# RWKV-6 attention with a gated feed-forward on one core: the input projections of the last two units made as one product of half matrices

## The chip, the core and the metric

The kernel runs on one core of a Trainium2 chip. The core has five engines that run side by side and wait for each other by semaphores: TensorE (matrix products; in profiles PE, and PEld for its loading of weights), VectorE (DVE), ScalarE (ACT), GpSimd (POOL) and SyncE (SP), which here only starts DMAs. TensorE reads from the on-chip memory SBUF and writes to the accumulators, PSUM[...]. The metric is the device time of one execution in microseconds; less is better.

## What is computed

Inputs r, k, v, w have the shape 4 (batch) x 8 (heads) x 768 (time) x 48. A recurrence over time gives y, and y, with the heads side by side, gives 3072 rows x of 384 numbers. They go through a feed-forward block with 2048 hidden features:

```python
for t in range(S):
    cur = np.einsum('bhd,bhe->bhde', u[None] * kt, vt)
    y[:, :, t] = np.einsum('bhd,bhde->bhe', rt, state + cur)
    state = wt[:, :, :, None] * state + np.einsum('bhd,bhe->bhde', kt, vt)
x = attn_out.transpose(0, 2, 1, 3).reshape(B * S, H * D)
h = x @ w_in                                             # 3072x384 by 384x2048
sp = np.maximum(h, 0.0) + np.log1p(np.exp(-np.abs(h)))   # softplus
g = h * erf(sp)
out = g @ w_out                                          # 3072x2048 by 2048x384
```

Everything is in 32-bit floats.

## The kernel before, in words

The work is cut into 12 steps (s = 0 to 11): 6 stretches of 128 time steps, each for two pairs of batches. A step makes the attention of 2 batches x 128 time steps; its 256 rows of x are called a unit and go through the feed-forward block behind it. For each unit there are

- the attention of its step. From step 5 on `attend_late` does it: products within a block of time by levels (`level_products`, L552, and `scale`, L328), their use on v (`from_own`, L584, in two halves, with the VectorE copy `seen`, L593, between them), the state products (`state_part`, L659), the sum `middle` (L736), and the part that comes through the state (`through_state`, L610). The last one copies the result from the accumulator `y` to the tile xT (ScalarE, L618 and L639) and moves 6 small pieces of it by DMA (L645). xT holds the unit's 384 inputs in three parts of 128 rows, 256 tokens wide.
- the input projection, `hidden` ("H"): 16 feature tiles of 128, three whole-array products each (L1027, weights 128x128 from w_in_sb, 256 columns), two feature tiles per accumulator, copied to h by ScalarE (L1036). 8 pieces of 6 products.
- the gating, in chunks of four feature tiles: softplus ("s", L983) and erf ("e", L987) on ScalarE, each with a load of its function table (1.28 us), and the product on VectorE ("m", L992).
- the output projection, `project_fast` ("P"), made by seven products of half matrices in place of eight: h and w_out are seen as 2x2 blocks. `blend` ("S", L1112 to L1118) makes four sums of blocks of h on VectorE; seven pieces of 8 products (L1135, 192 columns) follow, with evictions on ScalarE (L1141, L1146, L1149) and VectorE (L1155, L1160) and two output DMAs.

The order is written by hand: every engine performs its instructions in the order in which the program gives them out. In step s a "P" stands for the next output product of unit s - 3 and an "H" for the next piece of unit s - 1; they are put between the parts of the attention. `run_late` reads strings of such tokens; `LATE` holds those of step 11 by stage (front, near, 0, 1, 2, 3, 4). In step 11 the stages up to 1 hold the output products of unit 8, stage 2 the blend of unit 9, and stages 3 and 4 the 8 pieces of unit 10's input projection. Behind step 11 come the attention's last products, the output products of unit 9, the input projection of unit 11, and then the output products of units 10 and 11:

```python
from_own(s - 1, ready[s - 1][0], 1)
fence()
run_late(s, "s P")
from_own(s - 1, ready[s - 1][0], 0)
through_state(s - 1, xTs[s - 1])
run_late(s, "m ey m P s P P ep m P P P S H H s H ey m H H s H ep m H H")
run_late(s + 1, "s P ey m P s P P ep m P P P S")
run_late(s + 2, "P P P P P P P")
```

Products with fewer than 128 rows and columns (L552, L584, L610, L659) use a quarter of the array each: which rows follows from the partitions of the operands, which columns from the partitions of the result.

Of the kernel before, what the change touches and what calls it, by code (L numbers as in the profile page):

```python
# [11 lines left out]
FP32 = mybir.dt.float32  # L12
# [49 lines left out]
def kernel(  # L62
# [240 lines left out]
    def rows(e, n=D):  # L303
        return slice(e * EP, e * EP + n)
# [293 lines left out]
    def through_state(s, xT):  # L598

        c, in_t, _, _, S, _, _ = parts_of(s)  # L600
        for h, state in enumerate((S, middle)):
            if not (c or h):
                continue
            t = slice(h * HC, (h + 1) * HC)
            for j, q in ((0, 2), (1, 2), (1, 0), (0, 0)) if not s else np.ndindex(NJ, NP // 2):
                q = q if not s else 2 * q
                for e in range(NE):
                    for p in (q + e, q + 1 - e):
                        n = j * NP + p
                        nc.tensor.matmul(  # L610
                            y[at(e, p), e, p // 2, j, t],
                            lhsT=state[rows(e), n, :],
                            rhs=(in_t[:, 0, n] if s else first_pair(0, n))[rows(e), t],
                            start=False, stop=True, skip_group_check=True,
                        )

        y3 = att.tile([P, UNIT], FP32, name="y3", bufs=1)
        nc.scalar.copy(y3[:].rearrange("p (j t) -> p j t", j=NJ), y[:, 1, 1])  # L618
        parts = y[:, 0, 0], y[:, 0, 1], y[:, 1, 0]
        by_kk = [xT[:, kk, :].rearrange("p (j t) -> p j t", j=NJ) for kk in range(KT)]  # L620
        if not s:

            def hop():
                for kk in range(KT):
                    nc.tensor.matmul(
                        parts[kk], lhsT=apart[:, kk],
                        rhs=y3[:].rearrange("p (j t) -> p j t", j=NJ),
                        start=False, stop=True, skip_group_check=True,
                    )
                for kk in range(KT):  # L630
                    nc.scalar.copy(by_kk[kk], parts[kk])
                stages["l"](3, xT[:, KT - 1, 0:1], True)
                stages["l"](4)
                load_w(2)

            turns["hop"] = hop
            return
        for kk in range(KT):
            nc.scalar.copy(by_kk[kk], parts[kk])  # L639
        by_scalar = {(kk, 1) for kk in range(KT) if s <= DIRECT}  # L640
        for kk in range(KT):
            n = D // KT
            for e in range(NE):
                queue = nc.scalar if (kk, e) in by_scalar else nc.sync
                queue.dma_start(  # L645
                    out=xT[e * EP + D : (e + 1) * EP, kk, :],
                    in_=y3[e * EP + kk * n : e * EP + (kk + 1) * n, :],
                )
# [424 lines left out]
    def mix_weights():  # L1073
# [9 lines left out]
            engine.tensor_tensor(out=of, in0=a, in1=b, op=op)  # L1083
        yield

    blends, lanes = {}, {}

    def quarter(of, what):
# [8 lines left out]
    def blend(of, *parts):  # L1097

        if of not in blends:
            if of < n_steps - 1:  # L1100
                tiles = [room[:, n] for n in (1, 2, 3)]
            else:
                two = att.tile([P, 2, JP, C], FP32, name="rk1", bufs=1)
                one = ins.tile([P, JP, C], FP32, name="w")
                tiles = [x.rearrange("p n t -> p (n t)") for x in (two[:, 0], two[:, 1], one[:])]
            s1, s2, s4 = (x.rearrange("p (f t) -> p f t", t=C) for x in tiles)
            blends[of] = s1, s2, quarter(of, "21"), s4
        s1, s2, s3, s4 = blends[of]
        a = {what: quarter(of, what) if what not in lanes else lanes[what] for what in ("11", "12", "22")}
        for part in parts or (1, 2, 4, 3):  # L1110
            if part == 1:
                nc.vector.tensor_add(s1, s3, a["22"])  # L1112
            elif part == 2:
                nc.vector.tensor_sub(s2, s1, a["11"])
            elif part == 3:
                nc.vector.tensor_sub(s3, a["11"], s3)
            else:
                nc.vector.tensor_sub(s4, a["12"], s2)  # L1118

    def project_fast(s, gs):  # L1120
# [47 lines left out]
                nc.sync.dma_start(out=out[i * NJ, c, :, part], in_=o[0][:, part])  # L1168
        yield

    xTs, hids, projs = {}, {}, {}
    gated = [[] for _ in range(n_steps)]

# [28 lines left out]
    def in_order(s, k):  # L1202
# [3 lines left out]
        for what in order[k]:  # L1206
# [12 lines left out]
            "S2 S3 H k12y S4 H F", "s H ep m H H F G s H H H ep",  # L1219
        ),  # L1220
        n_steps - 1: (
            "s P", "m", "ey P m s P P ep P", "m P P", "S", "H H", "s H ey m H H s H ep H H"
        ),
    }
    USUAL = (
# [4 lines left out]
    def run_late(s, tokens, following=None):  # L1230

        for what in tokens.split():
# [5 lines left out]
                piece(hids, s - 1)  # L1238
            elif what == "F":
                next(following, None)  # L1240
            elif what == "G":
                mixing.send(nc.gpsimd)
            elif what == "s":
# [39 lines left out]
    with tc.manual_schedule(  # L1283
# [74 lines left out]
        s = n_steps  # L1358
        from_own(s - 1, ready[s - 1][0], 1)
        fence()  # L1360
        run_late(s, "s P")
        from_own(s - 1, ready[s - 1][0], 0)
        through_state(s - 1, xTs[s - 1])
        run_late(s, "m ey m P s P P ep m P P P S H H s H ey m H H s H ep m H H")
        run_late(s + 1, "s P ey m P s P P ep m P P P S")
        run_late(s + 2, "P P P P P P P")


# [94 lines left out]
```

## Time and profile before

| | us |
|---|---|
| median of 3 runs | 589.04 (588.01 to 589.31) |
| the profiled execution | 591.17 |
| its span, first to last instruction | 589.3 |
| TensorE busy | 582.3 |
| VectorE busy | 434.6 |
| ScalarE busy | 361.2 |
| GpSimd busy | 273.4 |
| one unit's input projection (96 records) | 20.9 |

The page of the profile gives busy time by engine, and the chain of work that ended last; the trace behind it can be asked for the instructions of any stretch in order of time. A row of such an answer gives the start in us from the first instruction, the duration, the engine, the line of the program, the operation, the tile that is written and those that are read, for TensorE the part of the array that is used (rows*columns), the shape, and how many instructions the row stands for. In square brackets stands the idle time of the engine ahead of it and what ended it; "issue" means that no other instruction did. A 32-bit product on TensorE leaves two records of loading and two of multiplying. The ends of products are modelled, so that rows overlap; starts are measured.

### The profile page before, as it was taken

What the parts mean: (1) busy time and instruction counts of PE and PEld (TensorE: products, weight loads), DVE (VectorE), ACT (ScalarE), POOL (GpSimd) and SP (SyncE); (2) the same over time, 40 slices, a digit from 0 to 9 for tenths busy, and PEclk for the clock granted to TensorE, in tenths of its full rate; (3) what the DMA queues carried; (4) which work ended last, traced back from release to release, by engine and by line L of the source; (5) the groups of instructions that cost most, each with busy time, mean ns of one, the idle gap of its engine ahead of it and who ended that gap; (6) DMA issues with size and microseconds to landing.
All of it is one profiled execution on the core that took longest, in us unless ns stands there. A gap on an engine that the chain in (4) does not pass through costs nothing.

```text
span 589.3 us, 16635 instructions
## 1 busy us (share of the span) xinstructions
PE 582.3 (99%) x7256; PEld 500.6 (85%) x7256; DVE 434.6 (74%) x523; ACT 361.2 (61%) x474; POOL 273.4 (46%) x313
## 2 busy tenths in 40 slices
PE   8899999999999999999999999999999999999997
PEld 6688887688668768998998998998898898898997
DVE  6775886899996899799799799799799525023140
ACT  3567878644544598756766766766766754746720
POOL 4557381702398479569369369369359000000000
PEclk9899999999999999999999999999999999999999
DMA  7577572440432514234334334333331300000000
GB/s 258 185 258 292 187 238 61 172 153 10 143 110 103 135 45 160 46 133 153 65 128 159 65 128 150 73 125 116 73 121 42 73 21 14 3 19 15 1 27 28
DMA packets 54081, 63.24 MB, mean 107 GB/s; under 512 B 35160, under 2 KB 40568, under 8 KB 52984
## 3 DMA queue, kind: packets, MB, share of 16 engines
q1 hardware_dynamic: 53624, 61.98, 33.2%
q8 instruction: 57, 0.93, 0.7%
q10 hardware_dynamic: 384, 0.20, 0.1%
q14 instruction: 16, 0.13, 0.1%
HBM read 52.39 MB, written 8.69 MB: 104 GB/s over the span
## 4 chain that ended last, share of the span: by engine, by line
PE 89%; DVE 8%; issue 1%; DMA 1%; POOL 0%; SPq 0%; DVEq 0%; POOLq 0%
PE m L1027 40%; PE m L1135 28%; PE m L1059 6%; PE pp L552 6%; PE y L584 2%; PE pp L659 2%; PE y L610 2%; DVE in L328 2%; PE m L862 1%; DVE words L467 1%; DVE rk L463 1%; DMA rest<-in_w_rows 1%; DVE sums L453 1%; PE pp L871 1%; DVE h L1016 1%
## 5 line engine op out<-in xcount | busy, mean ns | idle before, releaser
L1027 PE MATMUL m<-xT,w_in_sb 128*128 128x256 f32 x1152 | 256.8, 382 | 0.0
L1027 PEld LDWEIGHTS m<-xT,w_in_sb 128*128 128x128 f32 x1152 | 216.4, 190 | 30.5 <-ACT h L1036 0.3
L1036 ACT COPY h<-m 128x512 f32<-128x512 f32 x96 | 55.5, 578 | 83.1 <-PE m L1027 83.1
L328 DVE TENSOR_TENSOR in<-in,tot_sb 128x1024 f32<-128x1024 f32 (+1 forms) x55 | 74.6, 1357 | 15.9 <-PE pp L552 13.7
L463 POOL TENSOR_TENSOR rk<-words 128x528 f32<-128x528 f32 (+3 forms) x28 | 42.4, 1515 | 91.2 <-DVE sums L453 80.8
L467 POOL TENSOR_TENSOR words<-words,rest 128x528 f32<-128x528 f32 (+10 forms) x77 | 78.1, 1015 | 6.0
L1059 PE MATMUL m<-w_out_sb,h 128*128 128x384 f32 x192 | 64.3, 491 | 0.0
L1059 PEld LDWEIGHTS m<-w_out_sb,h 128*128 128x128 f32 x192 | 35.7, 190 | 23.5
L1135 PE MATMUL m<-mixed,h 128*128 128x192 f32 x288 | 51.1, 331 | 0.0
L983 ACT ACT_TABLE_LOAD x36 | 46.2, 1283 | 2.8 <-issue 2.1
L1135 PE MATMUL m<-w_out_sb,h 128*128 128x192 f32 x272 | 47.5, 329 | 0.0
L1135 PEld LDWEIGHTS m<-mixed,h 128*128 128x128 f32 x288 | 46.6, 190 | 0.9
L987 ACT ACT_TABLE_LOAD x36 | 46.2, 1283 | 1.6 <-DVE room L1118 1.1
L1135 PEld LDWEIGHTS m<-w_out_sb,h 128*128 128x128 f32 x272 | 44.3, 190 | 0.4
L1135 PE MATMUL m<-w_out_sb,room 128*128 128x192 f32 x256 | 44.2, 326 | 0.0
L552 PEld LDWEIGHTS pp<-in 48*64 48x64 f32 (+1 forms) x2368 | 33.4, 126 | 11.6 <-issue 6.0
L1135 PEld LDWEIGHTS m<-w_out_sb,room 128*128 128x128 f32 x256 | 42.0, 190 | 0.0
L992 DVE TENSOR_TENSOR h<-h,y 128x1024 f32<-128x1024 f32 x17 | 20.7, 1216 | 28.3 <-ACT y L987 28.1
L402 POOL TENSOR_TENSOR tot_sb<-tot_sb 128x256 f32<-128x256 f32 (+4 forms) x50 | 37.1, 742 | 3.8
L983 ACT ACTIVATE room<-h 128x1024 f32<-128x1024 f32 x36 | 38.1, 1057 | 0.4
L992 DVE TENSOR_TENSOR h<-h,pp 128x1024 f32<-128x1024 f32 x19 | 23.1, 1213 | 19.5 <-ACT pp L987 19.5
L552 PE MATMUL pp<-in 48*64 48x32 f32 (+1 forms) x2368 | 37.1, 212 | 0.2 <-DVE in L328 0.2
(147 smaller groups left out, 830.5 us busy)
## 6 DMA issues: line engine op xcount, KB each, us to landing
in<-in_rkw SPq DMA_DIRECT2D x8, 1024.0 KB, 5.7
words<-in_moe_w_in SPq DMA_DIRECT2D x16, 384.0 KB, 6.1
words<-in_moe_w_out SPq DMA_DIRECT2D x16, 384.0 KB, 5.8
words<-in_rk_rows SPq DMA_DIRECT2D x8, 768.0 KB, 6.4
w<-in_rkw SPq DMA_DIRECT2D x11, 512.0 KB
v<-in_v SPq DMA_DIRECT2D x12, 384.0 KB, 5.7
out<-o SPq DMA_DIRECT2D x23, 192.0 KB, 2.9
in<-in_rkw SPq DMA_DIRECT2D x7, 512.0 KB, 5.8
```

Of the source, the lines that this page charges most:

```text
L328: nc.vector.tensor_mul(halves, halves, view(tots[level - 1], 0, [[1, n], [2, nb], [0, half]]))
L402: nc.gpsimd.tensor_mul(new, pair[:, :, 0], pair[:, :, 1])
L463: engine.tensor_mul(terms[n], r[:, :, n:], k[:, :, : near - n])
L467: engine.tensor_mul(k[:, :, :m], k[:, :, :m], w[:, :, n : n + m])
L552: nc.tensor.matmul(to, lhsT=rk(1, n)[rows(e), s0 : s0 + m], rhs=right, start=True, stop=True,)
L983: nc.scalar.activation(sp_room, chunks[0], AF.Softplus)
L987: nc.scalar.activation(at, sp_room, AF.Erf)
L992: nc.vector.tensor_mul(h, h, at)
L1027: nc.tensor.matmul(ps[:, ff, :], lhsT=w_in_sb[:, g * FG + f + ff, kk * P : (kk + 1) * P], rhs=xT[:, kk, :], start=kk == 0, stop=kk == KT - 1,)
L1036: nc.scalar.copy(h[:, f : f + FT, :], ps[:])
L1059: nc.tensor.matmul(ps[j][:], lhsT=gs[g][:, f, j * C : (j + 1) * C], rhs=w_out_sb[:, g * FG + f, :], start=g + f == 0, stop=g == NG - 1 and ...
L1135: nc.tensor.matmul(to, lhsT=a[:, f], rhs=b[:, f], start=start and f == 0, stop=f == FG - 1, skip_group_check=True,)
```

## The change

Units 10 and 11 are projected together. Seen as 2x2 blocks, the inputs of w_in are halved (two halves of 192 rows), its features are halved (two groups of 8 tiles), and the tokens are the two units. The four block results are then made from seven products of blocks in place of eight, with sums of blocks made ahead:

- A half of the inputs is one of the first two 128-row parts and 64 rows of the third. A product of one pair of feature tiles is so made of 2 whole-array matmuls (L1281 of the new program) and 4 matmuls of 64 rows by 64 features on the four quarters of the array (L1288), all 256 columns wide. There are 7 x 4 of them.
- `join_weights` moves 64-row parts of w_in to the other rows (4 DMAs, SBUF to SBUF) and makes four sums of weight blocks on VectorE, one in step 11's near stage, one in stage 1 and two behind the step. `swap_rows` moves 64 rows of each unit's third part to the other rows (2 DMAs a unit), and `join_tokens` makes four sums of token blocks on VectorE.
- `hidden_of_two` makes the products, with two accumulators of `products` and the one named y, and puts the results together by ScalarE copies and VectorE sums. Gating is done by half chunks (`activate_pair`), with up to four activations between loads of a table.
- Step 11 holds no "H" and no blend any more. The blend of unit 9 comes behind the step, and of unit 9's seven output products the last two come behind the joint products. The six pieces of unit 11's xT are sent in another order, the third part first.

```diff
@@ -638,7 +638,7 @@
         for kk in range(KT):
             nc.scalar.copy(by_kk[kk], parts[kk])
         by_scalar = {(kk, 1) for kk in range(KT) if s <= DIRECT}
-        for kk in range(KT):
+        for kk in range(KT) if s < n_steps - 1 else np.roll(range(KT), 1):
             n = D // KT
             for e in range(NE):
                 queue = nc.scalar if (kk, e) in by_scalar else nc.sync
@@ -1083,6 +1083,11 @@
             engine.tensor_tensor(out=of, in0=a, in1=b, op=op)
         yield
 
+    def half_room(name, shape):
+        t = wide.tile(shape, I32, name=name, bufs=3 if name == "words" else 2)
+        t = t[:].rearrange("p a b two -> p (a b two)" if len(shape) == 4 else "p a b -> p (a b)")
+        return t.bitcast(FP32)
+
     blends, lanes = {}, {}
 
     def quarter(of, what):
@@ -1097,8 +1102,10 @@
     def blend(of, *parts):
 
         if of not in blends:
-            if of < n_steps - 1:
+            if of < n_steps - 2:
                 tiles = [room[:, n] for n in (1, 2, 3)]
+            elif of == n_steps - 1:
+                tiles = [half_room("words", [P, 2, DM, 2])[:, : FG * C] for _ in range(3)]
             else:
                 two = att.tile([P, 2, JP, C], FP32, name="rk1", bufs=1)
                 one = ins.tile([P, JP, C], FP32, name="w")
@@ -1168,6 +1175,175 @@
                 nc.sync.dma_start(out=out[i * NJ, c, :, part], in_=o[0][:, part])
         yield
 
+    def join_weights():
+
+        n = FG * P
+        tiles = [half_room("words", [P, 2, DM, 2]) for _ in range(3)]
+        s1, s2, s4 = (
+            (
+                t[:, :n].rearrange("p (f m) -> p f m", m=P),
+                t[:, n : n + n // 2].rearrange("p (f m) -> p f m", m=P),
+            )
+            for t in tiles
+        )
+        moved = [
+            half_room("rest", [P, 2, DM])[:, : n // 2].rearrange("p (f m) -> p f m", m=P)
+            for _ in range(2)
+        ]
+        a_rows, b_rows = (rows(e, EP) for e in range(NE))
+        thirds = [slice(kk * P, (kk + 1) * P) for kk in range(KT)]
+        for g in range(NG):
+            even, odd = (slice(g * FG + n, (g + 1) * FG, 2) for n in range(2))
+            nc.sync.dma_start(out=moved[g][a_rows], in_=w_in_sb[b_rows, even, thirds[2]])
+            nc.sync.dma_start(out=moved[g][b_rows], in_=w_in_sb[a_rows, odd, thirds[2]])
+
+        def whole(g, half):
+            return w_in_sb[:, g * FG : (g + 1) * FG, thirds[half]]
+
+        def rest(g, half, e):
+
+            if half == e:
+                return w_in_sb[rows(e, EP), g * FG + e : (g + 1) * FG : 2, thirds[2]]
+            return moved[g][rows(e, EP)]
+
+        def block(g, half):
+            return whole(g, half), [rest(g, half, e) for e in range(NE)]
+
+        def tile_of(t):
+            return t[0], [t[1][rows(e, EP)] for e in range(NE)]
+
+        s1, s2, s4 = (tile_of(t) for t in (s1, s2, s4))
+        a11, a12, a21, a22 = (block(g, half) for g in range(NG) for half in range(2))
+        turns["joint weights"] = {
+            "11": a11, "12": a12, "22": a22, "s1": s1, "s2": s2, "s3": a21, "s4": s4
+        }
+        yield
+        for out_, a, op, b in (
+            (s1, a21, ALU.add, a22), (s2, s1, ALU.subtract, a11),
+            (s4, a12, ALU.subtract, s2), (a21, a11, ALU.subtract, a21),
+        ):
+            nc.vector.tensor_tensor(out=out_[0], in0=a[0], in1=b[0], op=op)
+            for e in range(NE):
+                nc.vector.tensor_tensor(out=out_[1][e], in0=a[1][e], in1=b[1][e], op=op)
+            yield
+
+    def swap_rows(of):
+
+        if "swapped" not in turns:
+            t = att.tile([P, NH, HC], FP32, name="own")
+            t = t[:].rearrange("p n t -> p (n t)").rearrange("p (i t) -> p i t", t=UNIT)
+            turns["swapped"] = {n_steps - 2 + i: t[:, i] for i in range(2)}
+        to = turns["swapped"][of]
+        for e in range(NE):
+            nc.sync.dma_start(out=to[rows(e, EP)], in_=xTs[of][rows(1 - e, EP), KT - 1, :])
+
+    def join_tokens():
+
+        def block(of, half):
+            swapped = turns["swapped"][of]
+            return xTs[of][:, half, :], [
+                (xTs[of][:, KT - 1, :] if half == e else swapped)[rows(e, EP)] for e in range(NE)
+            ]
+
+        room_of = ins.tile([P, 2, JP, C], FP32, name="in")
+        room_of = room_of[:].rearrange("p x n t -> p (x n t)").rearrange("p (i t) -> p i t", t=UNIT)
+        t1, t2, t3, t4 = (
+            (room_of[:, 2 * i], [room_of[rows(e, EP), 2 * i + 1] for e in range(NE)])
+            for i in range(4)
+        )
+        b11, b21, b12, b22 = (
+            block(of, half) for of in (n_steps - 2, n_steps - 1) for half in range(2)
+        )
+        for out_, a, b in ((t1, b12, b11), (t2, b22, t1), (t4, b21, t2), (t3, b22, b12)):
+            nc.vector.tensor_sub(out_[0], a[0], b[0])
+            for e in range(NE):
+                nc.vector.tensor_sub(out_[1][e], a[1][e], b[1][e])
+        turns["joint tokens"] = {
+            "11": b11, "21": b21, "22": b22, "t1": t1, "t2": t2, "t3": t3, "t4": t4
+        }
+
+    def hidden_of_two():
+
+        one, two = n_steps - 2, n_steps - 1
+        h11, h21 = (hid.tile([P, FG, UNIT], FP32, name="h")[:] for _ in range(NG))
+        h12 = room[:, 2:4].rearrange("p i n -> p (i n)").rearrange("p (f t) -> p f t", t=UNIT)
+        h22 = ins.tile([P, 2, JP, C], FP32, name="in")
+        h22 = h22[:].rearrange("p x n t -> p (x n t)").rearrange("p (f t) -> p f t", t=UNIT)
+        gated[one].extend((h11, h21))
+        gated[two].extend((h12, h22))
+        m0 = y[:, :, 0].rearrange("p e j t -> p e (j t)")
+        low, high = (products([P, NE, 2, UNIT], n)[:, :, 0] for n in range(2))
+
+        def product(to, a, b, i, start):
+            whole, rest = turns["joint weights"][a]
+            tokens, rest_tokens = turns["joint tokens"][b]
+            for e in range(NE):
+                nc.tensor.matmul(
+                    to[:, e], lhsT=whole[:, 2 * i + e], rhs=tokens,
+                    start=start, stop=True, skip_group_check=True,
+                )
+            for e in range(NE):
+                for c in range(NC):
+                    m = slice(c * HC, (c + 1) * HC)
+                    nc.tensor.matmul(
+                        to[m, e], lhsT=rest[e][:, i, m], rhs=rest_tokens[e],
+                        start=False, stop=True, skip_group_check=True,
+                    )
+
+        pairs = FG // 2
+        for i in range(pairs):
+            f = slice(2 * i, 2 * i + 2)
+            product(low, "12", "21", i, True)
+            nc.scalar.copy(h11[:, f], low)
+            yield
+            product(m0, "11", "11", i, True)
+            nc.vector.tensor_add(h11[:, f], h11[:, f], m0)
+            chunks.append(h11[:, f])
+            yield
+            product(high, "s1", "t1", i, True)
+            nc.scalar.copy(h22[:, f], high)
+            yield
+            product(m0, "s2", "t2", i, False)
+            nc.vector.tensor_copy(h12[:, f], m0)
+            yield
+            product(low, "22", "t4", i, True)
+            nc.scalar.copy(h21[:, f], low)
+            yield
+            product(m0, "s3", "t3", i, False)
+            nc.vector.tensor_add(h21[:, f], h21[:, f], m0)
+            nc.vector.tensor_add(h22[:, f], h22[:, f], m0)
+            chunks.append(h21[:, f])
+            if i < pairs - 2:
+                chunks.append(h22[:, f])
+            yield
+            product(high, "s4", "22", i, False)
+            nc.vector.tensor_add(h12[:, f], h12[:, f], high)
+            if i < pairs - 2:
+                chunks.append(h12[:, f])
+            elif i == pairs - 1:
+                chunks.extend(h[:, 2 * i - 2 : 2 * i + 2] for h in (h12, h22))
+            yield
+
+    slots = {"next": 0, "u": [], "v": []}
+
+    def activate_pair(what):
+
+        if what == "u":
+            h = chunks.pop(0)
+            i, k = divmod(slots["next"] % 4, 2)
+            slots["next"] += 1
+            n = FT * UNIT
+            at = room[:, i, k * n : (k + 1) * n].rearrange("p (f t) -> p f t", t=UNIT)
+            nc.scalar.activation(at, h, AF.Softplus)
+            slots["u"].append((h, at))
+        elif what == "v":
+            h, at = slots["u"].pop(0)
+            nc.scalar.activation(at, at, AF.Erf)
+            slots["v"].append((h, at))
+        else:
+            h, at = slots["v"].pop(0)
+            nc.vector.tensor_mul(h, h, at)
+
     xTs, hids, projs = {}, {}, {}
     gated = [[] for _ in range(n_steps)]
 
@@ -1219,7 +1395,7 @@
             "S2 S3 H k12y S4 H F", "s H ep m H H F G s H H H ep",
         ),
         n_steps - 1: (
-            "s P", "m", "ey P m s P P ep P", "m P P", "S", "H H", "s H ey m H H s H ep H H"
+            "W s P", "m X w", "ey P m s P P ep P", "m P P w", "", "", ""
         ),
     }
     USUAL = (
@@ -1238,6 +1414,22 @@
                 piece(hids, s - 1)
             elif what == "F":
                 next(following, None)
+            elif what == "Q":
+                piece(projs, s - 2)
+            elif what == "J":
+                next(turns["joint"])
+            elif what == "W":
+                turns["join weights"] = join_weights()
+                next(turns["join weights"])
+            elif what == "w":
+                next(turns["join weights"])
+            elif what in "uvz":
+                activate_pair(what)
+            elif what == "X":
+                swap_rows(s - 1)
+            elif what == "T":
+                join_tokens()
+                turns["joint"] = hidden_of_two()
             elif what == "G":
                 mixing.send(nc.gpsimd)
             elif what == "s":
@@ -1358,11 +1550,15 @@
         s = n_steps
         from_own(s - 1, ready[s - 1][0], 1)
         fence()
-        run_late(s, "s P")
+        run_late(s - 1, "S Q w w")
         from_own(s - 1, ready[s - 1][0], 0)
         through_state(s - 1, xTs[s - 1])
-        run_late(s, "m ey m P s P P ep m P P P S H H s H ey m H H s H ep m H H")
-        run_late(s + 1, "s P ey m P s P P ep m P P P S")
+        run_late(s, "X P P P P T")
+        run_late(s, "J J J J J u J u u J")
+        run_late(s, "J u v J J v J z z J v v J z u u u J z")
+        run_late(s, "J u v J J v J z z J v v J z u u J z")
+        run_late(s, "J J u v J J z v J z v J z u v J z P P S")
+        run_late(s + 1, "P s P ey P m s ep P m P P P S")
         run_late(s + 2, "P P P P P P P")
```

## The prediction

> **What bounds the kernel now.** I read the page first (busy shares, the slices, the chain that ended last), then the order of time of TensorE over the last 100 us, then of VectorE and ScalarE in the same stretch.
>
> ```profile
> PE 582.3 (99%) x7256; PEld 500.6 (85%) x7256; DVE 434.6 (74%) x523; ACT 361.2 (61%) x474; POOL 273.4 (46%) x313
> ...
> PE 89%; DVE 8%; issue 1%; DMA 1%; POOL 0%; SPq 0%; DVEq 0%; POOLq 0%
> ```
>
> ```profile
> 487.50 20.99 PE L1027 MATMUL m<-xT,w_in_sb 128*128 128x256 f32 x96
> 508.42 0.67 PE L584 MATMUL y<-own,v 64*48 64x64 f32 x32
> 509.01 2.87 PE L1135 MATMUL m<-w_out_sb,h 128*128 128x192 f32 x16
> 511.81 0.66 PE L584 MATMUL y<-own,v 64*48 64x64 f32 x32
> 512.29 0.63 PE L610 MATMUL y<-in,s 48*48 48x64 f32 x32
> 512.74 0.63 PE L610 MATMUL y<-in,middle 48*48 48x64 f32 x32
> 513.30 2.87 PE L1135 MATMUL m<-mixed,h 128*128 128x192 f32 x16
> 516.00 2.76 PE L1135 MATMUL m<-w_out_sb,room 128*128 128x192 f32 x16
> 518.60 2.76 PE L1135 MATMUL m<-mixed,room 128*128 128x192 f32 x16
> ...
> 529.00 20.88 PE L1027 MATMUL m<-xT,w_in_sb 128*128 128x256 f32 x96
> 549.72 2.76 PE L1135 MATMUL m<-w_out_sb,h 128*128 128x192 f32 x16
> ```
>
> In the page TensorE is busy 99% of the span. In the second view (start, duration, engine, line, operation, size of the array used, shape, records) every row starts before the one above has ended: from the projection of unit 10 (487.50) to the end nothing holds TensorE, and its granted clock is 1.00 there. So the end moves by what the change adds to or takes from TensorE, plus waits that are new. Each f32 matmul leaves two records, two passes over the array. The rows also give unit prices, by differences of starts, since the ends are modelled:
> - A whole-array pass of 256 columns: (549.72 - 529.00) / 96 = 0.2158 us. One unit's input projection is 96 such passes.
> - Eight output products' matmuls (16 passes of 192): 518.60 - 516.00 = 2.60 us, 1.69 ns a column and matmul.
> - Quarter-array matmuls: L610 takes 512.74 - 512.29 = 0.45 us for 16 matmuls of 64 columns, 28 ns each, where the whole array would need 64 x 1.69 = 108 ns. So four quarters do run side by side at full rate.
> - The same rows show a price for going from the whole array to quarters and back. L1135 started at 509.01 and L584 behind it at 511.81: 2.80 us in place of 2.60. L584 takes 0.48 before L610 where L610 takes 0.45 before L610; the last L610 takes 0.56 before L1135; and that L1135 takes 2.70 before the next (513.30 to 516.00), not 2.60.
>
> **What the skill says of it.** The Trainium skill, TensorEngine Tiling (Array Packing), Key Properties, says that tiles work independently, but that changing the tiling mode, not just the tile, drains TensorE; it gives no price. The trace agrees with both halves, and prices the second. In
>
> ```profile
> 508.42 0.52 PEld L584 LDWEIGHTS y<-own,v 64*48 64x48 f32 x32 [0.33 <-issue]
> ...
> 511.81 0.52 PEld L584 LDWEIGHTS y<-own,v 64*48 64x48 f32 x32 [0.23 <-issue]
> ```
>
> the weight loader, which elsewhere runs ahead under the matmul before, stands 0.33 and 0.23 us at "issue", waiting for no instruction that the profile knows. Record by record, going in, the first load starts 94 to 97 ns after the last whole pass has been streamed (its start plus its columns at 2.4 GHz), and the second row of four quarter passes starts 94 ns after the first where 56 ns is the rhythm: 38 ns for a load that nothing covers. Coming out, the first whole load starts 91 to 95 ns after the last quarter pass is streamed (up to 122 after some L552 shapes), four quarters start over 20 ns, and the second whole pass comes 267 ns behind the first in place of 162: 105 ns of open load. This holds at practically all of some 130 changes of mode in the trace, under other waits at the rest. TensorE: Matmul & The Clock Gate, LDWEIGHTS, prices a load by its columns over 1.2: 40 ns for 48 columns, 107 for 128, against the 38 and 105 here; for 64 columns I take 51 (38 x 64/48).
> So one round trip costs 94 + 51 + 20 + 92 + 105 = 362 ns, call it 0.36 us. The forecast goes by this sum, not by the rule alone.
>
> **The change part by part.**
> 1. *Removed.* 2 x 96 passes of 256 columns, unit 10's in step 11 and unit 11's in the tail: 192 x 0.2158 = 41.43 us. With unit 10's projection gone, the state products (L659) are followed by L584, quarters behind quarters: one round trip less, 0.35 (48-column weights).
> 2. *Added on TensorE.* Seven products for each of four pairs of feature tiles, 28. Each is 2 whole-array matmuls (4 passes) and 4 quarter matmuls of 64 x 64 weights, in the same order of rows and columns as L610, with 256 columns: 8 quarter passes four abreast, the time of 2 passes. 6 x 0.2158 = 1.295 us; x 28 = 36.26. That is the intended gain of 5.17 us. But every product goes from whole array to quarters and back: 28 x 0.36 = 10.1 us. Net 36.26 + 10.1 - 41.43 - 0.35 = **+4.6 us**. A product then lasts 1.65 us, a pair of feature tiles 11.6. That four quarters stay abreast at 256 columns is not shown; L610, L584 (4 x 56 ns) and L552 show it at 64 and fewer, where starts of the four lie 7 ns apart, so a quarter doesn't wait for its neighbour's second pass. From below it can't be cheaper than 2 passes, from above it is 4 (two abreast). I take 2. The open load and the drain don't depend on the columns of the pass before (94 ns behind 192, 256 and 384 alike).
> 3. *The order around step 11.* Unit 9's output product Q comes behind L659 and L584, then the second L584, L610, four more products of unit 9, then the 28. The second L584 waits for the copy "seen" (L593) on VectorE. Ahead of it stand there, by the after-order of instructions: L1155, L1160 (done 487.32 by the row before), the second part of the weight sums (1.22 for 128x1024, and two of 64x512 at up to 0.69, the 128x512 row of L328: 2.6), "middle" L736 1.11, L593 0.17: 491.2. TensorE: L659 ends 487.5, L584 0.45, drain, Q 2.7, drain: 490.9. **A wait of 0.35 us**; between 0 and 0.9.
> 4. *VectorE from there.* Blend of unit 9, 4 x 1.22 = 4.9; two parts of weight sums 5.2; token sums 4 x (128x256, and two of 64x256; at 1.03 ns an element over a fixed 0.16 from 1.22 and 0.69: 0.43 each) = 5.2. Ends 491.2 + 15.3 = 506.5, its first token sum at 502.6. TensorE after L610 is at 492.8, four products to 503.6, and the first product that needs a token sum is the third: 506.9. Covered by 4 us. The first sums in the near stage delay kT (L718, 468.7) by 2.6, against L659 at 486.65: covered.
> 5. *DMAs.* Four moves of weight rows on SP ahead of step 11's L645, whose sources and room are free by about 461 (the last POOL user of "rest" is done 456.5); needed at 468.8. Two swaps per unit behind the six L645 (0.6 apart, landing 1.8 later): for unit 11 about 494 to 500, needed at 502.6 and at the latest 506.9. While SP waits for the landing only output stores are behind. Nothing on the path; if the swaps were 7 us late they would be.
> 6. *Evictions and gating in the 28.* ScalarE per pair: 3 copies at 0.58, 8 half-size activations at about 0.6 (a 128x512 copy is 0.58), 2 table loads at 1.28: 9.1 of 11.6 us. VectorE: 5 from PSUM and 4 products at 0.69: 6.2. Each accumulator is written again two products after its reader starts. In the last pair the last gate product ends 2.4 us behind the last matmul, covered by unit 9's last two products (5.2). No wait; below nothing impossible, since TensorE is the bound.
> 7. *The tail.* Unit 10's products run with ScalarE order copy, softplus, erf, copy, softplus, erf, copy. From the end of the 28: first product done 7.8; copy 0.3, load and softplus 2.35, load and erf 2.3, copy by 13.6, softplus 15.9, erf 18.25, copy L1149 18.6. The sixth product overwrites what that copy reads and is due at 18.2: **0.45 us** (0 to 0.9). The two blends are ready 3 us ahead.
>
> Sum: 4.6 + 0.35 + 0.45 = +5.4. The profiled execution took 591.17 (span 589.3, 1.9 around it): 596.6 for such a one. The median of the runs shown, 589.04, lies 2.1 below the profiled one; I add the 5.4 to it: **594.4 us**.
>
> **The rivals.**
> - *The mode change is hidden* (faster). If the loader took its tiles ahead, the 10.1 us would go: 589.04 - 41.43 - 0.35 + 36.26 + 0.8 = 584.3. For it: quarter passes here last 213 ns, longer than in any row, and TensorE's queue has work for both. Against: the 94 ns start when the stream ends, whatever the length. It decides below 0.17 us a round trip, half of the smallest sum seen (0.35).
> - *Quarters only two abreast* (slower still). 28 x 2 x 0.2158 = 12.1 more: 606.5. For it: two rows of the array share output partitions, at a longer pass than shown. Against: L610 does exactly that at 28 ns.
> - *A new wait is the bound*: VectorE's 15 us queue after the last step or ScalarE's 9.1 of 11.6 us, if contention stretched them by a third: some 3 us, 597.5. Against: 4 us and 2.5 us of cover.
> - That the change does not do what it says: the instruction order shows 28 groups of 2 and 4 matmuls in place of 96, so no.
>
> **How the numbers follow.** The likeliest, with waits of 0 to 1.8 and 0.31 to 0.41 a round trip, 78%: 592.3 to 596.8. New wait 7%, two abreast 5%: both slower. Hidden 8%, partly hidden so that it about cancels 2%. The range 591.5 to 599 leaves out two abreast and hidden. A difference under 0.2% (1.2 us) is about what measuring this kernel can't tell from none. Slower 0.90, same 0.02, faster 0.08.
>
> **What would show it.** In the profile after: a product's start to the next some 1.65 us (1.30 if the rival is right, 2.08 if two abreast); four quarter matmuls starting within 20 ns; the loader standing at "issue" ahead of each group of quarters and each whole one; the 28 from the first L1281 to the next output product some 46 us; TensorE waiting 0.3 us for L593 and 0.4 us for L1156 (the old L1149), nowhere for token sums. I am wrong if quarters of 256 columns load or drain otherwise than those of 64.

## The result and the profile after

The changed kernel takes 593.68 us (median of 6 runs, 593.00 to 595.59), the kernel before 588.33 (6 runs, 587.99 to 589.31): the ratio is 1.0094, with a 95% interval of 1.0075 to 1.0114. Run once more beside other kernels it took 593.90 against 588.11 (1.0102, 1.0080 to 1.0123). The forecast was 594.4, and +5.4 over the kernel before; measured are +5.35 and +5.8.

The profiled execution took 593.0 us, with a span of 591.2. That is only 1.9 more than the span shown of before, because the two executions differ ahead of the change: that of before carries half the TensorE clock for 7 us near its start (mean clock 0.994), that of after does not (1.000), and its last state products (L659) start at 483.02 and not 486.65. So I compare from there on. The first row is of before, the second of after:

```profile
486.65 0.92 PE L659 MATMUL pp<-v,kT 64*48 64x48 f32 x32
...
483.02 0.88 PE L659 MATMUL pp<-v,kT 64*48 64x48 f32 x30
```

From the first of these L659 to the end of the span the kernel before takes 589.35 - 486.65 = 102.70 us, the changed one 591.21 - 483.02 = 108.19: +5.49. This "tail" is used for all runs below. It is the part that the change touches on TensorE, and it repeats to 0.01 us: 108.20 in the second profile of the changed kernel.

The page of the profile after, busy shares and chain, looks as before:

```profile
PE 583.8 (99%) x7400; PEld 486.4 (82%) x7400; DVE 464.2 (79%) x573; ACT 355.7 (60%) x478; POOL 271.7 (46%) x313
...
PE 83%; DVE 10%; ACT 2%; issue 2%; POOL 2%; DMA 1%; DVEq 0%; POOLq 0%; SPq 0%
```

TensorE is again "99% busy"; the drains between modes don't show in that figure, since the modelled end of a product reaches over them. They show in the starts. TensorE in order of time, the tail of the changed kernel:

```profile
487.51 0.66 PE L584 MATMUL y<-own,v 64*48 64x64 f32 x32 [0.32 <-DVE seen L593]
487.99 0.63 PE L610 MATMUL y<-in,s 48*48 48x64 f32 x32
...
499.50 1.03 PE L1281 MATMUL pp<-xT,w_in_sb 128*128 128x256 f32 x4
500.46 0.43 PE L1288 MATMUL pp<-own,rest 64*64 64x256 f32 x2
500.47 0.43 PE L1288 MATMUL pp<-xT,w_in_sb 64*64 64x256 f32 x2
500.72 0.38 PE L1288 MATMUL pp<-own,rest 64*64 64x256 f32 x2
500.74 0.38 PE L1288 MATMUL pp<-xT,w_in_sb 64*64 64x256 f32 x2
501.05 1.13 PE L1281 MATMUL y<-xT,w_in_sb 128*128 128x256 f32 x4
...
504.36 1.13 PE L1281 MATMUL y<-in,words 128*128 128x256 f32 x4
505.42 0.66 PE L1288 MATMUL y<-in,words 64*64 64x256 f32 x8
506.01 1.13 PE L1281 MATMUL pp<-in,w_in_sb 128*128 128x256 f32 x4
...
507.34 0.38 PE L1288 MATMUL pp<-in,rest 64*64 64x256 f32 x2
...
545.69 2.87 PE L1142 MATMUL m<-mixed,h 128*128 128x192 f32 x16
548.39 5.36 PE L1142 MATMUL m<-w_out_sb,h 128*128 128x192 f32 x32
...
564.48 2.87 PE L1142 MATMUL m<-mixed,h 128*128 128x192 f32 x16 [0.33 <-ACT o L1156]
```

The reader is to see three things. A product lasts 506.01 - 504.36 = 1.65 us, start to start, and all 28 take 545.69 - 499.50 = 46.19 us. From the first whole pass to the first quarter pass it is 1.06 us (504.36 to 505.42), where four whole passes take 0.86; and from the quarters to the next whole pass 0.59, where two ranks of quarter passes take 0.43 (a rank is four quarter passes that start within 20 ns; the eight of a product make two). And there are two idle times with a name, 0.32 behind L593 and 0.33 behind L1156, and no third.

The weight loader in the same stretch:

```profile
505.42 0.21 PEld L1288 LDWEIGHTS y<-in,words 64*64 64x64 f32 x8 [0.33 <-issue]
506.01 0.73 PEld L1281 LDWEIGHTS pp<-in,w_in_sb 128*128 128x128 f32 x4 [0.39 <-issue]
507.07 0.14 PEld L1288 LDWEIGHTS pp<-in,rest 64*64 64x64 f32 x2 [0.33 <-issue]
507.08 0.14 PEld L1288 LDWEIGHTS pp<-in,w_in_sb 64*64 64x64 f32 x2
507.12 0.14 PEld L1288 LDWEIGHTS pp<-in,rest 64*64 64x64 f32 x2
507.14 0.14 PEld L1288 LDWEIGHTS pp<-in,w_in_sb 64*64 64x64 f32 x2
507.66 0.73 PEld L1281 LDWEIGHTS y<-in,w_in_sb 128*128 128x128 f32 x4 [0.39 <-issue]
```

Ahead of every group it stands 0.33 or 0.39 us, 56 times in all: once into the quarters and once out of them in each product. (The trace puts some of these to an eviction that ended about then; most of them, as here, to "issue", to no instruction at all.) Within the quarters it runs ahead: all eight loads are issued by 507.14, while the second rank of passes starts only at 507.34.

### The profile page after: what moved, and what is told of

Read it like the earlier page. It is cut to its first block, busy times and chain, and to the rows that moved or that the text cites. A ratio compares the mean times of both kernels' runs of the same rounds, so it can differ in the third digit from the quotient of the medians.

```text
span 591.2 us, 17002 instructions
## 1 busy us (share of the span) xinstructions
PE 583.8 (99%) x7400; PEld 486.4 (82%) x7400; DVE 464.2 (79%) x573; ACT 355.7 (60%) x478; POOL 271.7 (46%) x313
## 4 chain that ended last, share of the span: by engine, by line
PE 83%; DVE 10%; ACT 2%; issue 2%; POOL 2%; DMA 1%; DVEq 0%; POOLq 0%; SPq 0%
PE m L1027 30%; PE m L1142 27%; PE m L1059 6%; PE pp L552 4%; PE pp L1281 3%; PE y L1281 2%; DVE in L328 2%; PE y L584 2%; PE pp L1288 2%; PE y L610 2%; PE pp L659 1%; PE m L862 1%; PE y L1288 1%; DVE words L467 1%; DMA rest<-in_w_rows 1%
## 5 line engine op out<-in xcount | busy, mean ns | idle before, releaser
L1027 PE MATMUL m<-xT,w_in_sb 128*128 128x256 f32 x960 | 214.7, 382 | 0.2 <-ACT h L1036 0.2
L1027 PEld LDWEIGHTS m<-xT,w_in_sb 128*128 128x128 f32 x960 | 179.9, 190 | 25.6 <-ACT h L1036 0.5
L328 DVE TENSOR_TENSOR in<-in,tot_sb 128x1024 f32<-128x1024 f32 (+1 forms) x55 | 76.1, 1384 | 15.4 <-PE pp L552 13.7
L1036 ACT COPY h<-m 128x512 f32<-128x512 f32 x80 | 46.4, 581 | 57.4 <-PE m L1027 57.4
L1142 PE MATMUL m<-mixed,h 128*128 128x192 f32 x256 | 45.8, 332 | 0.3 <-ACT o L1156 0.3
L1142 PE MATMUL m<-w_out_sb,h 128*128 128x192 f32 x256 | 44.8, 329 | 0.0
L1142 PEld LDWEIGHTS m<-mixed,h 128*128 128x128 f32 x256 | 41.2, 190 | 1.9 <-ACT o L1156 0.6
L1142 PE MATMUL m<-w_out_sb,room 128*128 128x192 f32 x240 | 41.5, 326 | 0.0
L463 POOL TENSOR_TENSOR words<-words 128x336 f32<-128x336 f32 (+6 forms) x49 | 35.1, 717 | 3.8
L453 DVE TENSOR_REDUCE sums<-rk 128x14 f32<-128x672 f32 (+9 forms) x54 | 34.7, 703 | 0.0
L453 DVE TENSOR_REDUCE sums<-words 128x6 f32<-128x288 f32 (+8 forms) x66 | 26.9, 466 | 3.8 <-POOL words L463 3.6
```

The costliest lines, as they stand in the source:

```text
L328: nc.vector.tensor_mul(halves, halves, view(tots[level - 1], 0, [[1, n], [2, nb], [0, half]]))
L453: nc.vector.tensor_reduce(out=view(sums[:], n, [[near * (NEAR + 1), NEAR // near], [NEAR + 1, near - n]]), in_=terms[n], axis=mybir.AxisLi ...
L463: engine.tensor_mul(terms[n], r[:, :, n:], k[:, :, : near - n])
L1027: nc.tensor.matmul(ps[:, ff, :], lhsT=w_in_sb[:, g * FG + f + ff, kk * P : (kk + 1) * P], rhs=xT[:, kk, :], start=kk == 0, stop=kk == KT - 1,)
L1036: nc.scalar.copy(h[:, f : f + FT, :], ps[:])
L1142: nc.tensor.matmul(to, lhsT=a[:, f], rhs=b[:, f], start=start and f == 0, stop=f == FG - 1, skip_group_check=True,)
```

## The experiments

The theory: each change between the whole array and its quarters drains TensorE and leaves a load open, 0.36 us for going there and back, and 28 of these eat the gain. The rivals: quarter passes of 256 columns are slow or held up by evictions (then the order of the parts is of no account); or the place behind step 11 costs the time (then plain products there cost it too). A fourth, for later runs: ScalarE's throughput is the bound once products are short.

| run | time, us | before beside it | ratio (95%) | joint stretch | tail |
|---|---|---|---|---|---|
| kernel before | | 588.33 | | | 102.70 |
| changed, 28 round trips | 593.68 | 588.33 | 1.0094 (1.0075 to 1.0114) | 46.19 | 108.19 |
| 14 round trips | 589.56 | 588.94 | 1.0007 (0.9989 to 1.0024) | 41.28 | 103.18 |
| no quarters | 579.23 | 588.94 | 0.9847 (0.9822 to 0.9872) | 30.77 | 93.68 |
| two waits gone | 592.84 | 588.94 | 1.0077 (1.0054 to 1.0100) | 46.19 | 107.21 |
| plain in place | 597.59 | 588.94 | 1.0152 (1.0127 to 1.0178) | 50.72 | 112.00 |
| plain, better gating | 587.91 | 588.58 | 0.9990 (0.9980 to 1.0001) | 41.44 | 102.36 |
| 8 round trips | 589.09 | 588.58 | 1.0012 (1.0000 to 1.0024) | 41.20 | 103.21 |
| 8, no waits | 588.53 | 588.58 | 1.0000 (0.9987 to 1.0014) | 41.20 | 102.22 |
| 8, gating later | 587.16 | 588.11 | 0.9989 (0.9975 to 1.0003) | 40.12 | 101.15 |

"Joint stretch" is the time from the start of the first product of the input projections of units 10 and 11 to the start of the next output product.

### Half of the round trips

```diff
-            for e in range(NE):
...
+            both = (wholes, rests) if order["next"] % 2 == 0 else (rests, wholes)
+            order["next"] += 1
+            both[0](to, a, b, i, start)
+            both[1](to, a, b, i, False)
```

> The same 28 products, but every second one makes its four quarter matmuls first and its two whole-array ones behind them, so that quarters follow quarters and whole follow whole: 14 round trips of the array's mode in place of 28, all else alike. Theory (a round trip costs 0.36 us): 14 x 0.36 = 5.0 us less than the changed kernel, 588.7. Rival (products are long because quarter passes of 256 columns are slow, or evictions hold them up): no change, 593.7.

Every instruction of the changed kernel is there, and only the order within every second product is turned (`wholes` and `rests` hold the two halves of the old `product`). The joint stretch is 46.19 - 41.28 = 4.91 us shorter, 0.351 for each of the 14 round trips that are gone; the time falls by 4.1 us between the medians (4.7 when each is taken against the kernel before that ran beside it), and by 5.0 in the tail. TensorE in order of time shows it:

```profile
508.22 0.43 PE L1290 MATMUL pp<-in,rest 64*64 64x256 f32 x2
508.24 0.43 PE L1290 MATMUL pp<-in,w_in_sb 64*64 64x256 f32 x2
508.49 0.38 PE L1290 MATMUL pp<-in,rest 64*64 64x256 f32 x2
508.50 0.38 PE L1290 MATMUL pp<-in,w_in_sb 64*64 64x256 f32 x2
508.70 0.38 PE L1290 MATMUL y<-in,w_in_sb 64*64 64x256 f32 x2
508.72 0.38 PE L1290 MATMUL y<-in,rest 64*64 64x256 f32 x2
508.92 0.38 PE L1290 MATMUL y<-in,w_in_sb 64*64 64x256 f32 x2
508.93 0.38 PE L1290 MATMUL y<-in,rest 64*64 64x256 f32 x2
509.25 1.13 PE L1280 MATMUL y<-in,w_in_sb 128*128 128x256 f32 x4
510.21 1.03 PE L1280 MATMUL pp<-xT,words 128*128 128x256 f32 x4
```

(L1280 and L1290 are the L1281 and L1288 of the changed kernel.) The quarters of the second product follow those of the first without a break: its ranks start 0.21 and 0.22 us behind the rank before, the rhythm of a pass. So a rank of four quarter passes of 256 columns costs what one whole pass costs, and the rest of the price lies at the change of mode. The first rival falls.

### No quarters

```diff
-            for e in range(NE):
-                for c in range(NC):
...
-                    nc.tensor.matmul(
-                        to[m, e], lhsT=rest[e][:, i, m], rhs=rest_tokens[e],
```

> The 112 quarter matmuls are left out, so the last 64 rows of each half of the inputs don't enter the hidden features of units 10 and 11; evictions, sums and gating stay. Theory: both the passes (28 x 2 x 0.2158 = 12.1) and the round trips (10.1) go: 22.2 us less, 571.5, less by what ScalarE, with 9 us of work per pair of feature tiles against 6.0 of TensorE, then adds: about 3 us in each of four pairs, so 571 to 583. Rival (no price for the mode): 12.1 less at most, 581.6 or more, and the product period in the trace 0.43 us shorter instead of 0.79 where nothing waits.

The stretch is 46.19 - 30.77 = 15.4 us shorter, the time 14.5 us below the changed kernel's first median (15.1 when each is taken against the kernel before beside it), within the band that the theory gave and past what passes alone could give (12.1). Where nothing waits a product takes 0.86 us, start to start: 0.79 less, as the theory said. The first four products:

```profile
500.28 1.03 PE L1281 MATMUL pp<-xT,w_in_sb 128*128 128x256 f32 x4
501.15 1.03 PE L1281 MATMUL y<-xT,w_in_sb 128*128 128x256 f32 x4
502.01 1.03 PE L1281 MATMUL pp<-in,words 128*128 128x256 f32 x4
503.79 1.13 PE L1281 MATMUL y<-in,words 128*128 128x256 f32 x4 [0.75 <-DVE h L1293]
```

Of the stretch of 30.77, 6.6 us (30.77 less 28 x 0.863) are waits that the longer products had covered, with the loads that they leave open; the largest of them by name:

```profile
PE y L1281 <- DVE h L1293: 3.5, 4, 1.4
```

(who waited for whom, TensorE: total, times, longest). TensorE stands before the second use of the accumulator y, until VectorE has made the sum of the first two products, which needs ScalarE's copy of the first.

### The two waits

```diff
-            "W s P", "m X w", "ey P m s P P ep P", "m P P w", "", "", ""
+            "W s P", "m X w w", "ey P m s P P ep P", "m P P", "", "", ""
-        run_late(s + 1, "P s P ey P m s ep P m P P P S")
+        run_late(s + 1, "P s P ey P m s P ep m P P P S")
```

> The second part of the weight sums is moved from stage 1 to the near stage of step 11, and the second erf of the tail behind the fourth output product. Theory: the waits of TensorE for the copy seen (0.35) and for the copy L1156 (0.35 to 0.5) go: 0.7 to 0.8 us less, 592.9, and the 28 products unchanged at 1.65 us each. Rival (the move of the projection behind step 11 is what costs): more than 2 us less.

No wait of TensorE is left in the tail, the joint stretch is 46.19 as before, and the tail is 0.98 us shorter. That is a little more than the two idle times, since each of them also left a load or a drain open (the sixth product starts 0.49 us late for its 0.33 of idle time). The medians differ by 0.8 (by 1.45 when each is taken against the kernel before beside it). The rival's 2 us don't appear.

### Plain products in the same place

```diff
...
-        run_late(s - 1, "S Q w w")
+        run_late(s - 1, "S Q")
...
-        run_late(s, "X P P P P T")
-        run_late(s, "J J J J J u J u u J")
...
+        run_late(s, "P P P P P P")
+        run_late(s - 1, "H H H H s H ey H m H H s ep m")
+        run_late(s, "s ey m H H s H ep m H H s ey m H s H ep m H S")
```

> Units 10 and 11 projected behind the last step as in the changed kernel, but by the 96 whole-array matmuls of the kernel before (no weight sums, no token sums, no swaps). Theory: the place costs nothing and only the products do: as before, 588.3, within 0.5 either way (one round trip of the mode less, 0.35; the wait for the copy seen is gone with the weight sums). Rival (the place costs, step 11 without its filler leaves TensorE waiting): 591 to 594.

This missed by 9 us, and the cause lay in my own order of the gating. ScalarE in order of time:

```profile
526.61 1.28 ACT L983 ACT_TABLE_LOAD   x1
527.90 1.06 ACT L983 ACTIVATE room<-h 128x1024 f32<-128x1024 f32 x1
528.98 1.28 ACT L987 ACT_TABLE_LOAD   x1
530.27 1.03 ACT L987 ACTIVATE pp<-room 128x1024 f32<-128x1024 f32 x1
531.32 1.28 ACT L983 ACT_TABLE_LOAD   x1
532.61 1.06 ACT L983 ACTIVATE room<-h 128x1024 f32<-128x1024 f32 x1
533.68 1.28 ACT L987 ACT_TABLE_LOAD   x1
534.98 1.03 ACT L987 ACTIVATE y<-room 128x1024 f32<-128x1024 f32 x1
535.94 1.06 ACT L1036 COPY h<-m 128x512 f32<-128x512 f32 x2
```

Four activations with four loads, 9.3 us, stand ahead of the copy of h that frees an accumulator (535.94), and TensorE, with two accumulators, waits for it:

```profile
536.57 15.68 PE L1027 MATMUL m<-xT,w_in_sb 128*128 128x256 f32 x60 [5.42 <-ACT h L1036]
552.97 2.86 PE L1027 MATMUL m<-xT,w_in_sb 128*128 128x256 f32 x12 [0.72 <-ACT h L1036]
```

The wait is not the whole of it. The granted clock of TensorE is 0.50 from 534.8 to 541.6, and behind the long wait the passes start 0.427 us apart in place of 0.216 until it ends. The stretch is 9.3 us longer than with the gating spread out (next run): by the starts 5.6 are the long wait, 2.6 the passes at half the clock with the first open load, and 1.1 the shorter waits. That the wait brought the clock down is not shown by a run of its own. All five executions of this kernel have a mean clock of 0.994, while the run without quarters, with waits of at most 1.4 us, keeps 1.00 there. The run says nothing of the place. With the same products and the gating spread out,

```diff
-        run_late(s - 1, "H H H H s H ey H m H H s ep m")
-        run_late(s, "s ey m H H s H ep m H H s ey m H s H ep m H S")
-        run_late(s + 1, "s P ey m P s P P ep m P P P S")
+        run_late(s - 1, "H H s H ey m H H s H ep m H H")
+        run_late(s, "s H ey m H H s H ep m H H s H ey m H S")
+        run_late(s + 1, "s P ep m P s P P ey m P s P ep m P S")
```

> The plain 192 whole-array passes behind the last step again, but with the gating spread evenly: no more than two activations between two copies of h (in the last such run four of them with their table loads stood ahead of a copy, and TensorE waited 6.9 us for it). Theory (the place costs nothing): as before, within 0.5 us. Rival: 2 us or more slower, with TensorE waiting in step 11.

it is 0.9990 of the kernel before, 0.7 us less, its tail 0.34 us shorter, which is one round trip of the mode. No wait of TensorE is left in it. The place costs nothing, and the second rival falls.

### Eight round trips

```diff
+            work(i, "R1 W1" if i else "W1 W2 W3 R1")
...
+            work(i, "W2 W3 R2" if i else "R2")
...
+            work(i, "R3")
...
+            work(i, "R5 R4 W4")
...
+            work(i, "W5")
...
+            work(i, "W7 W6 R6")
...
+            work(i, "R7")
```

W and R are the whole-array part and the quarters of product 1 to 7 of a pair of feature tiles.

> The same 28 products with the same accumulators, sums and evictions, but within each seven the whole-array parts and the quarter parts are put in groups (whole 1, 2, 3; quarters 1, 2, 3, 5, 4; whole 4, 5, 7, 6; quarters 6, 7 and those of the next first): 8 round trips in place of 28. Theory at 0.351 a round trip (the value that the run with 14 gave: 46.19 - 41.28 over 14): the stretch of the joint products is 20 x 0.351 = 7.0 us shorter, 39.2 us, if ScalarE, now with 9.0 us of work per 9.8 us, keeps up; up to 2 us more if it does not. Time against the kernel before: 5.3 - 7.0 = 1.7 us less, up to even. Rival (only half of the price is the mode, the rest comes with any quarter pass): no further gain over the run with 14.

> The run with 8 round trips, and with it the two waits moved out of the way as in the run before (the second weight sum to the near stage, the second erf of the tail one product later). Theory: 0.7 to 0.8 less than with 8 round trips alone, 2.5 us less than the kernel before, ratio 0.9958. Rival (ScalarE is the bound once the products are short): the same as with 8 round trips alone.

> As the run with 8 round trips and no waits at the ends, with the gating products of VectorE put behind the last sum of each seven, and in the last seven the copy of the third product ahead of the activations. Theory: of the 2.1 us by which the stretch was longer than its passes and 8 round trips (36.26 + 2.8 = 39.1), 0.5 (TensorE behind ScalarE's copy) and 0.6 (the third whole part behind a sum that stood behind a gating product) go and 0.8 to 0.9 (the fourth quarters behind the sum of the first two products, four times) stays: 40.1 us, 1.1 less, ratio to the kernel before 0.998. Rival (ScalarE's throughput is the bound of the stretch, whatever the order): 41.2 as before.

The first gave a stretch of 41.20 and a time 0.5 us above the kernel before. The stretch is 2.1 us over the 39.1 of its passes and round trips (28 x 1.295 + 8 x 0.351), at the far end of what I had allowed for ScalarE. The second came out even with the kernel before and not 2.5 us faster, mostly for the same 2.1 us. But ScalarE's throughput was not the cause: with the gating products of VectorE behind the last sum, and one copy ahead of the activations,

```diff
-        run_late(s, "J u v J J v J z z J v v J z u u u J z")
-        run_late(s, "J u v J J v J z z J v v J z u u J z")
-        run_late(s, "J J u v J J z v J z v J z u v J z P P S")
+        run_late(s, "J u v J J v J z z J v v J u u u J z z")
+        run_late(s, "J u v J J v J z z J v v J u u J z z")
+        run_late(s, "J J J u v J v z J v z J u J v z z P P S")
```

the stretch is 40.12, as forecast, with no less work for ScalarE (busy 355.5 us against 355.3). What stays over is in the view of who waited, weight loader, in this last run:

```profile
PEld y L1290 <- issue: 2.3, 7, 0.3
PEld y L1290 <- DVE h L1316: 1.9, 4, 0.5
PEld y L1280 <- issue: 1.5, 4, 0.4
PEld pp L1280 <- issue: 1.2, 3, 0.4
```

Four times the fourth product's quarters wait for VectorE's sum of the first two; by the starts they come 0.36 us late once and 0.25 three times, 1.1 us together, which is what stays over the 39.1. This version takes 587.16 us against 588.11. Its tail is 1.55 us shorter than that of the kernel before and 7.05 shorter than that of the changed one. It beats the changed kernel clearly. That it beats the one before is not established by the times: the interval of its ratio reaches 1.0003, since what lies ahead of the tail starts the last L659 anywhere from 482.6 to 486.6 us in the profiles.

> The changed kernel once more beside the others on the same chip: 5.0 to 5.5 us over the kernel before.

It took 5.8 us more than the kernel before beside it, a little over what was expected, with the same joint stretch (46.19) and the same tail.

## Why the prediction was right

- *Removed, 41.43 us, and one round trip.* The rows of before give 508.42 - 487.50 = 20.92 and 549.72 - 529.00 = 20.72, together 41.64, with the first row holding a part of the round trip (an open load and a drain, 0.2). L584 now follows L659 without a drain, and plain products in the new place show that round trip by itself: the tail is 0.34 shorter, where 0.35 was forecast.
- *Added, 36.26 us of passes.* Four quarters of 256 columns do run abreast: they start within 20 ns, and the second rank 266 to 267 ns behind the first, of which 216 are the pass. This was the step with the widest bounds (up to 12.1 us), and the run with every second product turned settles it.
- *Added, 28 round trips at 0.36, 10.1 us.* Record by record in the changed kernel, from start to start and against the 215.8 ns of a whole pass: 309 ns from the last whole pass to the first quarter pass, 93 over; 266.5 to the second rank, 51 over; 20 of staggered starts; 306 from the last quarter pass to the next whole one, 90 over; and 320 to the second whole pass, 104 over. Together 358 ns. The prediction has 362, since its 94 and 92 take a pass of 256 columns to last 213 ns, where the starts give 216. By taking 14 of the round trips away it is 0.351. The first product follows whole passes and has no open load, so the sum is 36.26 + 28 x 0.358 - 0.10 = 46.18; measured are 46.19. The Trainium skill, TensorEngine Tiling (Array Packing), Key Properties, states that a change of mode drains TensorE; of the price measured here, about half is such a pause (93 and 90 of 358), and the rest are the loads that it leaves uncovered (51 and 104) and the stagger.
- *The wait for the copy "seen", 0.35, and for the copy ahead of the sixth output product, 0.45.* Both appeared where they were put, with 0.32 and 0.33 us of idle time; taking both away shortened the tail by 0.98, so together they were 0.2 larger than the forecast.
- *Covered.* VectorE's last token sum (L1260) ended at 502.2, or 505.9 on the clock of the execution before (3.63 later), against the 506.5 of the forecast. In the changed kernel TensorE waited for no token sum, no DMA and no eviction within the 28. So the rival of a new wait that becomes the bound falls too. The cover was needed: without the quarters TensorE did wait 3.5 us for an eviction.
- The rival of a hidden mode change (584.3) would have needed a product period of 1.30 us; it is 1.65. The rival of quarters two abreast needed 2.08.
- *The sum.* In the tail the change costs 5.49, of which 0.98 are the two waits and 4.51 the products, where 0.8 and 4.6 were forecast. That +5.4 was hit so closely is in part luck, since the two small errors point opposite ways; the mechanism does not rest on it. The absolute 594.4 starts from a median of 589.04 out of three executions, 0.7 above that of six.

What stays open: whether fewer than two round trips per pair of feature tiles can be had. The accumulator y takes the second, fourth and sixth product of a pair, one onto the other, and has to be read in between; more accumulators were not tried.

## What to carry to other kernels

Count the changes between whole-array and quarter-array products as work of their own: here 0.35 us there and back, as much as 1.6 passes of 256 columns, and no other work hid it. A scheme that saves one product in eight by halving matrices can lose its gain to them where the halves leave parts that need quarters of the array. Putting parts of one shape together, product behind product, wins the time back: with every second product turned this kernel came out even with the one before (1.0007), and with 8 round trips and the gating later it was 0.9 us ahead by the medians, which its interval does not tell from even. And where a wait is taken off TensorE, look at what stood behind it: evictions that held up nothing with 28 round trips, nor with 14, did with 8, where several products follow each other at the 1.3 us of their passes.

## What the runs showed of the hardware beyond that

The pause at a change of mode has no part that grows with the pass before. In the trace of before, the first quarter pass starts 256, 309 and 416 ns behind a whole pass of 192, 256 and 384 columns, where another whole pass starts 163, 216 and 323 ns behind it: 93 ns more each time. Two quarters that share array rows (and so read the same partitions) start 7 ns apart like any others. And a profile can call TensorE 99% busy while a fifth of a stretch (10 of 46 us) is pauses and open loads: the starts tell, not the busy share.
